# Rebuilding half of a reloaded operand on VectorE in a Strassen-Winograd MLP

## The chip, the cores and the metric

The kernel runs on one core of one Trainium2 chip. Five engines work side by side: TensorE (PE in the profile, with PEld for its weight loads), VectorE (DVE), ScalarE (ACT), GpSimd (POOL) and SyncE (SP, which here issues nearly all DMA transfers). The metric is the device time of one execution in microseconds; the figure shown for a kernel is the median over its runs.

## The reference

Two pre-normalized blocks with residuals, on x of 2048 x 1024 in bf16: a linear-attention block, and then a token-mixing MLP, whose matrix products run over the sequence. Only the MLP's second product matters here:

```
u = einsum("bsd,sf->bdf", h, w1) + b1     # first product, S = 2048 -> F = 3584
u = gelu(u)
y = einsum("bdf,fs->bds", u, w2) + b2     # second product, F = 3584 -> S = 2048
out = h + transpose(y)
```

## The kernel before

**Tiling.** The activations g = gelu(u) stay in SBUF, f16, split by feature tile: `gE` holds the even tiles of 128 features and `gO` the odd ones, each 14 tiles of 1024 columns (line 1532). The second product is done by the Winograd form of Strassen's scheme: seven products p1 to p7 of quarter size for each pair of 128-row output tiles, with moving operands that are sums of quarters of g. `gT2` is one of these, T3 = T2 - gE and T4 = gO - T2 (left columns) are two more. T2 lives in SBUF. T3 and T4 do not fit at once: they share two buffers, `gs0` and `gs1`, each half a T (7 tiles of 512 columns, 896 KB). They are computed once on VectorE (`derived`, line 1600), stored to DRAM (`parked`), and fetched again whenever needed (`reload`, line 1609).

**Two levels.** The outputs of two neighbouring pairs form a quad (class `Quad`). For a quad, products p1, p5, p2 and p3 are themselves done by a seven-product scheme (classes `Inner` and `Inner2`, i1 to i7, matmuls of 128x256), on the left operands of both pairs together; p6, p7 and p4 are done directly with matmuls of 128x512. The inner schemes leave short gaps in which their PSUM results are copied or summed, so `interleave` (line 536) weaves a direct product into each of them, in four portions: at the points named "b", "c", "2", "7", "third" and "end" it empties a list of late output steps or calls what the quad hung there.

**One quad** (`run2`, line 592) runs four interleaved stages in this order:
- in1 (inner product 1) with what is left of the last quad's p4, which reads the second half of T4. Its PE rows are psI for the inner product and psC<-gs for p4.
- in5 with p6 (rows psB<-gT). p6 accumulates onto a bank that ScalarE filled from the sums of in1 (line 523).
- in2 with p7, which reads T3 (psC<-gs).
- in3 with the first half of p4, which reads the first half of T4. `begin_next` starts the left-hand sums (rows is<-wq) for the next quad's in1.

Quads u = 1, 2 and 3 run this way; the second half of p4 of the last one runs after it, on its own.

**Order around the change.** `loads(u)` (line 1637) says when SyncE fetches what: T3 in "in3" and "in1", the first half of T4 at "p7", and its second half at "in2", just ahead of in3, right behind the two loads of the next quad's weights (`next2`, line 1630, called in line 647). A reload of a buffer waits until the products that read the old content are done. SyncE takes its queue strictly in order. VectorE and TensorE keep the order of the program in this part (class `Held`, line 222); ScalarE's order is left to the scheduler.

On VectorE, in3 consists of four sums of PSUM results into e (rows e<-psI,e; the second adds one result to both pairs) and two pairs of left-hand sums: that of in3 itself, and that of the next quad's in1. ScalarE then writes the two finished rows (line 487, wq<-e), to which POOL issues the output DMA.

In place, the even tiles of `gO` are altered early: the inner scheme's own sums (`sums2`) replace the right half of the left columns of every even tile by its difference with the left half (line 217, b12 - b11). T4 is made before that, at line 1674.

Of the kernel before, what the change touches and what calls it, by code (L numbers as in the profile page):

```python
# [10 lines left out]
P = 128  # L11
F32 = mybir.dt.float32
BF16 = mybir.dt.bfloat16
FP16 = mybir.dt.float16
ACT = mybir.ActivationFunctionType
ALU = mybir.AluOpType
# [14 lines left out]
def kernel(  # L31
# [12 lines left out]
    nc = tc.nc  # L44
# [5 lines left out]
    CW = min(BANK, D)  # L50
# [83 lines left out]
    NFP, NSP = NF // 2, NS // 2  # L134
    assert NDC == 2 and NF % 2 == 0 and NS % 2 == 0

    HW = CW // 2
# [23 lines left out]
    def load_w2(p, second, q=nc.sync):  # L161
        q.dma_start(
            (odd[p] if second else even[p % 2]),
            B_w2[:, p * 2 * P:(p + 1) * 2 * P].rearrange("(k two p) s -> p k two s", two=2, p=P)[:, :, second, :],
        )

    def first_w2(p):
        t = w_tile(wpool, WLEN)
        ots.extend(t[:, 2 * WH + o:2 * WH + o + CW] for o in (0, CW))
        even[p], odd[p] = w2_view(t[:, 0:WH]), w2_view(t[:, WH:2 * WH])  # L170
        odd[p + 4] = odd[p]
        for second in (0, 1):
            load_w2(p, second)
# [28 lines left out]
    dram = ctx.enter_context(tc.tile_pool(name="dram", bufs=1, space=bass.MemoryType.DRAM))  # L202
# [29 lines left out]
    dve, pe, act = Held(nc.vector), Held(nc.tensor), Held(nc.scalar, key="scalar")  # L232
# [267 lines left out]
    def share(sts):  # L500
        t = cpool.tile([P, 2, BANK], F32, tag="e", name="e1")
        for s, st in enumerate(sts):
            st.e = t[:, s, :]
        return t[:]

    class Quad:
# [85 lines left out]
        def run2(self, rest, nxt, load, sums, cut):  # L592
            sts = self.sts

            def starting():
                self.in1.sums(slice(2, 4))
                self.asums(5)
                self.in5 = self.inner(5)
                self.in5.sums(slice(0, 2))
                sts[0].asum(6)  # L600
                self.t1 = self.base("t1")
                for s, st in enumerate(sts):
                    st.begin(self.t1[:, s, :])

            def evac(s, dh, t):
                return lambda: sts[s].evac(0, dh, t[:, s, :])

            def every(*fs):
                return lambda: [f() for f in fs]

            def shared(st):
                self.late.pop(0)()
                dve.tensor_tensor(st.e[:], st.B[:], st.e[:], ALU.add)

            self.in1.behind = self.late
            self.interleave(
                self.in1, rest, {"b": starting, "7": lambda: self.in5.sums(slice(2, 4)), "third": sums[0]},
                (("b", None), ("7", None), ("end", None)),
            )
            load("in1")  # L620
            sts[1].asum(6)
            sums[1]()
            e = share(sts)
            in2 = Inner2(sts, 2, self.mov2, "i", self.add_to(self.t1), None)
            in2.sums(slice(0, 2))
            self.interleave(self.in5, self.steps(*[st.p6 for st in sts]), {
                "b": lambda: sts[0].asum(7), "2": lambda: sts[1].asum(7),
                "7": lambda: in2.sums(slice(2, 4)), "third": sums[2],
            })

            def third():
                self.in3 = Inner2(sts, 3, self.mov3, "i", self.add_to(e), None)
                shared(sts[0])
                evac(0, 0, self.t1)()
                self.in3.sums(slice(0, 2))

            self.interleave(in2, self.pieces(lambda st: st.p7_fill), {
                "b": every(lambda: sts[0].asum(3), sums[3]), "2": lambda: sts[1].asum(3),
                "7": lambda: load("p7"), "third": third,
                "end": lambda: self.late.append(evac(1, 0, self.t1)),  # L640
            }, (("7", None),))
            shared(sts[1])
            if cut is not None:
                sts[-1].split(cut)
                for st in sts:
                    st.fetch(1, 0)
            nxt = nxt()
            load("in2")
            p4 = self.pieces(lambda st: st.p4)

            def begin_next():
                if nxt is not None:
                    nxt.in1 = nxt.inner(1)
                    nxt.in1.sums(slice(0, 2))
                evac(0, 1, e)()

            self.interleave(self.in3, p4[:len(p4) // 2], {
                "b": lambda: self.in3.sums(slice(2, 4)), "third": begin_next,
                "end": lambda: self.late.append(evac(1, 1, e)),
            }, (("b", None), ("7", None)))  # L660
            load("in3")
            return p4[len(p4) // 2:], nxt
# [111 lines left out]
    with ExitStack() as actx:  # L774
# [21 lines left out]
        with ExitStack() as a1:  # L796
# [466 lines left out]
            for q in range(2, NVP):  # L1263
                for R in (KRun, VRun):
                    n = R(q)
# [28 lines left out]
            for b in range(NKB):  # L1294
                j0, n = b * KPB, min(KPB, ND - b * KPB)
# [237 lines left out]
    gO = gpool.tile([P, NFP, D], FP16, name="gO")  # L1533
# [44 lines left out]
    H2 = NFP // 2  # L1578
    gT2 = g2pool.tile([P, NFP, CW], FP16, name="gT2")
# [9 lines left out]
    parked = {}  # L1589

    def gs_tile(m, h):
        t = g2pool.tile([P, H2, CW], FP16, tag=f"gs{h}", name=f"gs{h}")
        gs[m, h] = t
        now = [gs.get((m, i)) for i in range(2)]
        gmov[m] = lambda k: now[k // H2][:, k % H2, :]
        return t

    gs = {}

    def derived(m, of):  # L1600
        def make(h):
            t = gs_tile(m, h)
            dve.tensor_tensor(t[:], *of(spans[h]), ALU.subtract)
            parked[m, h] = dram.tile([P, H2, CW], FP16, name=f"parked{m}{h}")
            nc.sync.dma_start(parked[m, h][:], t[:])

        return [partial(make, h) for h in range(2)]

    def reload(m, h):
        hd.dma_start(gs_tile(m, h)[:], parked[m, h][:])  # L1610

    make_t3 = derived(7, lambda sl: (gT2[:, sl, :], gE[:, sl, 0:CW]))
    make_t4 = derived(4, lambda sl: (gO[:, sl, 0:CW], gT2[:, sl, :]))
    first_w2(1)
    for p in (2, 3):
        odd[p] = odd[p + 4] = w2b.tile([P, NFP, 2 * P], BF16, tag=f"o{p}", name=f"w2o{p}")[:]
# [20 lines left out]
    def loads(u):  # L1637
        def load(at):
            last = 2 * u + 2 >= NSP
            if at == "in1":  # L1640
                if u == 1:
                    reload(7, 0)
                reload(7, 1)
                for p in (2 * u + 2, 2 * u + 3):
                    if 4 <= p < NSP:
                        load_w2(p, 1, hd)
            elif at == "p7":
                reload(4, 0)
            elif at == "in2":
                reload(4, 1)  # L1650
            elif at == "in3":
                if not last:
                    reload(7, 0)
        return load
# [70 lines left out]
```

## Time and profile before

| what | value |
|---|---|
| median of 5 runs | 563.22 us (562.88 to 564.05) |
| the profiled execution: its time, its span | 564.05 us, 562.2 us |
| TensorE busy | 552.6 us, 98% of the span, 3323 matmuls |
| VectorE busy | 427.9 us, 76%, 836 instructions |
| ScalarE busy | 291.1 us, 52% |
| granted TensorE clock | full in all slices |
| DMA moved | 77.92 MB, 139 GB/s over the span |
| reloads of gs from DRAM | 12 of 896 KB, median 5.1 us from issue to landing |
| stores of gs to DRAM | 4 of 896 KB, median 9.2 us |
| weight loads of the second product | 896 KB each, median 7.7 us (group of 12) |

The page gives busy time per engine; TensorE is the fullest. Times in the timeline are counted from the start of the span. A row of the timeline gives start, length, engine, source line (230 is the recording helper, under which most of this part stands), operation, output<-inputs, shape and how many instructions were merged; in brackets stands how long the engine was idle before it and what ended that. The second product runs from about 395 us on; quad 1 starts near 430, quad 2 near 473 and quad 3 near 514.

### The profile page before, as it was taken

The numbers are of one execution on the slowest core, as the hardware profiler recorded it, in microseconds if no ns is written. First come the engines' busy times: TensorE is split into PE (matmuls) and PEld (weight loads), VectorE is DVE, ScalarE is ACT, GpSimd is POOL, SyncE is SP. The second block draws the span as 40 slices with busy tenths as digits, with TensorE's granted clock in tenths as the row PEclk, the third lists the DMA queues.
The fourth block names the chain that finished last, engine by engine and source line by source line (L and its number), as shares of the span: only waits on it lengthen the run. The fifth ranks groups of instructions, "written<-read, shape, count | busy, mean of one in ns | idle before, by whom it ended". The sixth has DMA issues, their size and how long they took to land.

```text
span 562.2 us, 8812 instructions
## 1 busy us (share of the span) xinstructions
PE 552.6 (98%) x3323; PEld 316.3 (56%) x3339; DVE 427.9 (76%) x836; ACT 291.1 (52%) x617; POOL 28.1 (5%) x38
## 2 busy tenths in 40 slices
PE   8999999999999999999999999999999999998997
PEld 3444444454444444456666766666445666666665
DVE  6898888544777688889989789888997878648643
ACT  5747777766767877645546465564211312413313
POOL 1000000000000000000000000000002103102112
PEclk9999999999999999999999999999999999999999
DMA  9933342115774761103140340422969749849336
GB/s 294 305 75 76 76 91 41 19 40 199 221 207 130 245 196 76 75 1 103 50 149 22 129 151 1 150 66 66 234 203 273 220 139 294 209 128 275 87 92 134
DMA packets 84203, 77.92 MB, mean 139 GB/s; under 512 B 15666, under 2 KB 76096, under 8 KB 84160
## 3 DMA queue, kind: packets, MB, share of 16 engines
q1 hardware_dynamic: 79104, 72.76, 43.0%
q0 software_dynamic: 4384, 3.95, 4.8%
q10 hardware_dynamic: 672, 0.66, 0.4%
q8 instruction: 26, 0.43, 0.3%
q14 instruction: 17, 0.14, 0.1%
HBM read 61.62 MB, written 12.58 MB: 132 GB/s over the span
## 4 chain that ended last, share of the span: by engine, by line
PE 91%; DMA 5%; DVE 2%; SPq 1%; issue 1%; ACT 0%; DVEq 0%; ACTq 0%
PE psI L230 23%; PE acc_t L230 18%; PE psC L230 14%; PE psB L230 8%; PE psC L940 4%; PE psB L940 4%; DMA gs<-parked 4%; PE psA L940 4%; PE psB L342 2%; PE psA L342 2%; PE acc_t L1226 2%; PE psE L940 2%; PE psC L342 2%; PE acc_t L864 2%; DMA x_sb<-in_A_x_dram 1%; PE psA L230 1%
## 5 line engine op out<-in xcount | busy, mean ns | idle before, releaser
L230 PEld LDWEIGHTS <-is 128*128 128x128 f16 x736 | 71.8, 98 | 31.1 <-DVE hi L230 0.4
L230 PEld LDWEIGHTS <-sa 128*128 128x128 f16 x606 | 59.2, 98 | 27.1
L230 PEld LDWEIGHTS <-wq 128*128 128x128 bf16 (+1 forms) x496 | 48.5, 98 | 30.0 <-issue 2.9
L230 PE MATMUL acc_t<-wo_sb,pqT 128*128 128x512 f16 x256 | 55.6, 379 | 0.0
L484 POOL DMA_DIRECT2D out_dram<-wq x30 | 26.2, 935 | 528.8 <-ACT wq L487 498.1
L230 PE MATMUL acc_t<-xnT,wq_sb 128*128 128x512 bf16 x188 | 43.1, 379 | 0.2
L230 PEld LDWEIGHTS <-pqT 128*128 128x128 bf16 x256 | 25.0, 98 | 30.5 <-issue 0.6
L193 DVE TENSOR_SCALAR e_sb<-e_sb 128x512 bf16<-128x512 bf16 x64 | 18.6, 290 | 28.8 <-ACT e_sb L189 28.2
L230 DVE TENSOR_TENSOR t<-psI,t 128x256 f32<-128x256 f32 (+1 forms) x45 | 20.8, 475 | 22.2 <-PE psI L230 20.9
L189 ACT ACTIVATE e_sb<-acc_t 128x512 bf16<-128x512 f32 x40 | 23.9, 597 | 24.5 <-PE acc_t L230 12.0
L230 PE MATMUL psC<-gs,wq 128*128 128x512 f16 x140 | 34.1, 379 | 1.7 <-DMA gs<-parked 1.7
L940 PEld LDWEIGHTS <-xs 128*128 128x128 f16 x208 | 20.0, 98 | 23.3 <-DVE xs L926 1.3
L230 PEld LDWEIGHTS <-wq_sb 128*128 128x128 bf16 x192 | 18.5, 98 | 23.0 <-issue 1.3
L230 PE MATMUL psC<-hT,sa 128*128 128x512 f16 x112 | 31.2, 379 | 0.0
L230 PE MATMUL psI<-hi,is 128*128 128x256 f16 x200 | 30.0, 273 | 0.0
L230 PE MATMUL psB<-hT,sa 128*128 128x512 f16 x112 | 29.7, 379 | 0.0
L230 DVE BATCH_NORM_STATS2 hst<-acc_t 128x6 f32<-128x512 f32 x32 | 21.4, 692 | 9.1 <-ACT h_bf L230 8.9
L940 PE MATMUL psA<-wkv,xnT 128*128 128x512 bf16 x99 | 26.4, 379 | 0.3
L940 PEld LDWEIGHTS <-xnT 128*128 128x128 bf16 x156 | 15.3, 98 | 18.5 <-issue 0.2
L230 DVE TENSOR_TENSOR e<-psI,es 128x256 f32<-128x256 f32 x20 | 8.5, 425 | 21.8 <-PE psI L230 21.8
L230 PE MATMUL psC<-hT,wq 128*128 128x512 f16 x96 | 24.6, 379 | 0.0
L230 ACT CAST h_bf<-acc_t 128x512 bf16<-128x512 f32 x32 | 18.4, 582 | 11.8 <-PE acc_t L230 11.1
(227 smaller groups left out, 1090.5 us busy)
## 6 DMA issues: line engine op xcount, KB each, us to landing
wq<-in_B_w_dram SPq DMA_DIRECT2D x14, 1024.0 KB, 7.9
wq<-in_B_w_dram SPq DMA_DIRECT2D x12, 896.0 KB, 7.7
gs<-parked SPq DMA_DIRECT2D x12, 896.0 KB, 5.1
xr<-in_A_x_dram SPq DMA_DIRECT2D x16, 256.0 KB, 5.5
rdb<-rd_dram SPq DMA_DIRECT2D x32, 128.0 KB, 3.9
out_dram<-h_bf SPq DMA_DIRECT2D x16, 256.0 KB, 2.0
x_sb<-in_A_x_dram SPq DMA_DIRECT2D x15, 256.0 KB, 3.1
out_dram<-wq POOLq DMA_DIRECT2D x30, 128.0 KB, 5.8
```

Of the source, the lines that this page charges most:

```text
L189: pin(nc.scalar.activation(e_sb[:], src, ACT.Exp))
L193: pin(nc.vector.tensor_scalar(e_sb[:], e_sb[:], 1.0, PHI_EPS, ALU.min, ALU.add))
L230: return (lambda *a, **kw: pin(op(*a, **kw))) if self.always or getattr(Held, self.key) else op
L342: pe.matmul(ps[:, cols], lhsT=lhs[:, k, :], rhs=mv(k)[:, cols], start=(start and k == 0), stop=(k == self.nk - 1), skip_group_check=True,)
L484: nc.gpsimd.dma_start(to, ot[:, a:b], accum_op=ALU.add)
L864: mm = nc.tensor.matmul(pp[:, 0:CW], lhsT=xnT[:, kt, i * P:(i + 1) * P], rhs=wkv[:, kt, c * CW:(c + 1) * CW], start=(kt == 0), stop=(kt == ...
L940: pin(nc.tensor.matmul(ps[:], lhsT=lhs[:, k, :], rhs=rhs[:, k, :], start=(start and k == 0), stop=(k == hk2 - 1), skip_group_check=True,))
L1226: nc.tensor.matmul(qp[:, 0:SW], lhsT=wq_sb[:, kt, j * P:(j + 1) * P], rhs=xnT[:, kt, u * SW:(u + 1) * SW], start=(kt == 0), stop=(kt == ND ...
```

## The change

The second half of T4 is no longer stored and reloaded. For each quad it is recomputed on VectorE from `gO` and `gT2`, into the same buffer gs1, in two parts inside in3: tiles 7 to 9 at its point "2" and tiles 10 to 13 at its point "7". A part is one subtraction, and one addition that puts back gO's left half in the even tiles, which `sums2` had subtracted. The first half of T4 and both halves of T3 are reloaded as before. The first quad's T4, made at line 1674, is computed as before, and only its first half is stored.

```diff
             self.interleave(self.in3, p4[:len(p4) // 2], {
-                "b": lambda: self.in3.sums(slice(2, 4)), "third": begin_next,
+                "b": lambda: self.in3.sums(slice(2, 4)), "2": lambda: load("t4a"), "7": lambda: load("t4b"),
+                "third": begin_next,
                 "end": lambda: self.late.append(evac(1, 1, e)),
...
-    def derived(m, of):
+    def derived(m, of, park=(0, 1)):
         def make(h):
             t = gs_tile(m, h)
             dve.tensor_tensor(t[:], *of(spans[h]), ALU.subtract)
-            parked[m, h] = dram.tile([P, H2, CW], FP16, name=f"parked{m}{h}")
-            nc.sync.dma_start(parked[m, h][:], t[:])
+            if h in park:
+                parked[m, h] = dram.tile([P, H2, CW], FP16, name=f"parked{m}{h}")
+                nc.sync.dma_start(parked[m, h][:], t[:])
...
+    def remake_t4(second):
+        t, k = gs[4, 1], H2 + second * H2 // 2
+        n = NFP - k if second else H2 // 2
+        o = slice(k - H2, k - H2 + n)
+        dve.tensor_tensor(t[:, o, :], gO[:, k:k + n, 0:CW], gT2[:, k:k + n, :], ALU.subtract)
+        k += k % 2
+        even_k = slice(k - H2, o.stop, 2)
+        dve.tensor_tensor(
+            t[:, even_k, HW:CW], t[:, even_k, HW:CW], gO[:, k:H2 + o.stop:2, 0:HW], ALU.add,
+        )
...
-    make_t4 = derived(4, lambda sl: (gO[:, sl, 0:CW], gT2[:, sl, :]))
+    make_t4 = derived(4, lambda sl: (gO[:, sl, 0:CW], gT2[:, sl, :]), (0,))
...
             elif at == "in2":
-                reload(4, 1)
+                gs_tile(4, 1)
+            elif at in ("t4a", "t4b"):
+                remake_t4(at == "t4b")
```

## The prediction

> **What bounds the kernel.** I read the page first: TensorE (PE) is busy 98% of the span, and the chain that ended last lies on PE for 91% of it. So only a hole in PE's own stream can be won. Then I asked who PE waits for from 395 us on, in the second MLP product, the only part that the change touches. The answer is one line (total, times, longest):
>
> ```profile
> PE psC L230 <- DMA gs<-parked: 2.7, 2, 1.7
> ```
>
> Two waits for reloads of gs, and nothing else. The timeline of PE shows where (start, length, idle before):
>
> ```profile
> 473.17 0.93 PE L230 MATMUL psI<-gE,wq 128*128 128x256 f16 x7
> 475.13 1.02 PE L230 MATMUL psC<-gs,w2o 128*128 128x512 f16 x4 [1.03 <-DMA gs<-parked]
> 475.99 0.93 PE L230 MATMUL psI<-gi,is 128*128 128x256 f16 x7
> ...
> 513.89 0.93 PE L230 MATMUL psI<-gE,wq 128*128 128x256 f16 x7
> 516.50 1.02 PE L230 MATMUL psC<-gs,wq 128*128 128x512 f16 x4 [1.68 <-DMA gs<-parked]
> 517.36 0.93 PE L230 MATMUL psI<-gi,is 128*128 128x256 f16 x7
> ```
>
> The psC groups are the first four steps of product 4 on the **second half of T4**, woven into the next quad's first inner product. Idle in brackets leaves out PE's pipeline, so I count from starts. The chain has 14 matmuls of 128x256 in 1.53 us, so seven take 0.765 us, and psC could start at 473.17 + 0.765 = 473.94 and at 513.89 + 0.765 = 514.66. It starts **1.19 and 1.84 us** later: 3.03 us are open. The last quad's second half is used at its end, with no wait on a reload.
>
> Why the reload is late shows on SyncE's queue:
>
> ```profile
> 461.95 2.64 SPq L230 DMA_DIRECT2D wq<-in_B_w_dram  x2
> 464.65 8.28 SPq L230 DMA_DIRECT2D gs<-parked  x2
> ```
>
> It is issued at 464.65, behind two weight loads of 896 KB of which one had just left; the chain of waits gives it 10.43 us, and 11.09 us a quad later. Reloads with no weight load just ahead of them land in 4.6 to 5.6 us.
>
> **What goes.** Three reloads and one store of 896 KB, and two PE waits. By the Trainium skill ("DMA: Bandwidth & Descriptors", Anatomy of one DMA; Rules for kernel authors) a transfer costs some 2.0 us + bytes/436e3, and is to be issued early and waited for late. Its fit, made for another DMA path, gives 4.1 us as an estimate for 917,504 bytes: landed at 468.8, five us early, nothing to win, and the change would only load VectorE. The trace has 10.43 and 11.09 us under load, so I take the 3.03 us. The store (issued after 424) delays no PE instruction: PE has no wait between 395 and 475. SyncE loses four issues of about 0.33 us; its other loads keep their order and mostly wait for PE, so nothing there is won.
>
> **What comes.** Per quad, four VectorE (DVE) subtractions and additions, of 1,536, 256, 2,048 and 512 half-precision elements, in the third inner product. The order of the built program shows the first two right behind the e sum of 468.43, the other two behind the second sum of the pair at 469.78, and PE's order unchanged. The same operands were subtracted once already, in f16 throughout:
>
> ```profile
> 420.25 2.03 DVE L1603 TENSOR_TENSOR gs<-gO,gT 128x3584 f16<-128x3584 f16 x1 [0.68 <-PE psC L342]
> ```
>
> Groups by shape give 0.618 us for 896 and 1.083 for 1,792, also where a source is cut in runs of 256 (gO<-gO 1.092): 0.519 ns an element and 0.153 us fixed. So 0.95, 0.29, 1.22, 0.42 us. What counts is when the next one starts:
>
> ```profile
> 468.43 0.42 DVE L230 TENSOR_TENSOR e<-psI,e 128x256 f32<-128x256 f32 x1
> 469.78 1.22 DVE L230 TENSOR_TENSOR e<-psI,e 128x512 f32<-128x512 f32 x2 [0.94 <-PE psI L230]
> 471.96 0.42 DVE L230 TENSOR_TENSOR e<-psI,e 128x256 f32<-128x256 f32 x1 [0.95 <-PE psI L230]
> 472.43 0.63 DVE L230 TENSOR_TENSOR is<-wq 128x896 f16<-128x896 bf16 x1
> 473.09 0.63 DVE L230 TENSOR_TENSOR is<-is,wq 128x896 f16<-128x896 f16 x1
> 473.63 0.42 DVE L230 TENSOR_TENSOR e<-psI,e 128x256 f32<-128x256 f32 x1
> 473.97 0.62 DVE L230 TENSOR_TENSOR is<-wq 128x896 f16<-128x896 bf16 x1
> 474.50 0.62 DVE L230 TENSOR_TENSOR is<-wq,is 128x896 f16<-128x896 bf16 x1
> ...
> 480.18 0.42 DVE L230 TENSOR_TENSOR t<-psI,es 128x256 f32<-128x256 f32 x1 [0.74 <-PE psI L230]
> ...
> 481.59 0.42 DVE L230 TENSOR_TENSOR t<-psI,es 128x256 f32<-128x256 f32 x1
> ```
>
> The is of 474.50 starts 0.09 before the end of the one ahead; that of 473.09, which reads what 472.43 wrote, 0.03 after. The additions read what the subtractions wrote, so part one takes 0.95 + 0.03 + 0.29 - 0.08 = 1.19 and part two 1.22 + 0.03 + 0.42 - 0.08 = 1.59: **2.78 us a quad**. The skill ("VectorE: DVE Perf Modes", The DRAIN you can't avoid) says the next operation starts only when the pipe is empty, without overlap: the full durations and gaps would be 0.2 more, 2.94. The rows overlap; I take 2.78, with 2.3 (elements alone) and 2.94 as ends.
>
> **Who waits for it.** First, PE for T4 itself: part two ends near 472.7, wanted at 473.94. Second, what is queued behind on VectorE:
> - The two inner sums of 469.78 move to 469.97 and 470.8; PE's last inner group at 472.40 needs the second, done by 471.2.
> - The sum of 471.96 moves to 472.7 and the is pair to 473.05 and 473.7, done by 474.35. PE wants it at 474.80, after four psC steps of 0.216 us.
> - ScalarE (ACT):
>
> ```profile
> 473.36 1.50 ACT L487 ACTIVATE wq<-e,b_sb 128x512 bf16<-128x512 f32 x2 [5.56 <-DMA out_dram<-wq]
> 474.76 0.36 ACT L270 COPY psI<-psI 128x256 f32<-128x256 f32 x1
> ...
> 482.09 0.38 ACT L523 COPY psB<-t 128x256 f32<-128x256 f32 x1 [1.08 <-DVE t L230]
> ```
>
> L270 now runs behind both output evacuations, and PE's next inner group needs it. With that order PE could start only at 475.2 and 0.4 us would go. In the new order the second evacuation stands behind L270: first one 473.36 to 474.08, L270 474.18 to 474.54, before 474.80. Cost nothing.
> - The tightest: the sum at 481.59 and L523 behind it feed the product-6 matmul:
>
> ```profile
> 483.50 2.10 PE L230 MATMUL psB<-gT,sa 128*128 128x512 f16 x9
> ```
>
> L523 ends at 482.47, so 1.03 us are spare; PE now comes 1.19 earlier. VectorE has idle 0.94 + 0.95 + 0.74, three lost overlaps of 0.08 and 0.12 before 472.43 = 2.99 us between 468.43 and 481.59. It takes the 2.78 and runs without a gap, 0.2 earlier at the end. 1.03 + 0.2 covers 1.19, with nothing to spare; allowing for semaphores I book 0.1 us of new wait. A quad later the idles are 0.94, 0.96, 0.60, 0.84, plus 0.32: 3.66 - 2.78 + 1.03 = 1.91 against 1.84, 0.05 booked. If the cover is gone, each 0.1 us more on VectorE costs 0.1 us at each of the two places.
> - Last quad: sums wait for PE 0.94, 0.96 and 0.99 us, 3.1 with overlaps, more than 2.78; the last sum (555.48) stays in place, and the first evacuation (554.51) ends by 556.0, before the next starts. Cost nothing.
>
> **Sum.** 3.03 - 0.15 = 2.9 us off the span of 562.2. The profiled execution took 564.05, 1.85 outside the span, which stays; the median of the five runs is 563.22. 563.22 - 2.9 = **560.3 us**.
>
> **Rivals.**
> 1. VectorE's unbroken queue becomes the bound at the product-6 matmul. For it: no margin. If the four cost 0.5 us more (contention, waits between them), 1.0 comes back: 561.3.
> 2. Another wait takes the hole: the first evacuation's output buffer (its wait above is 5.56 us on an output DMA) or the weight load that ends at 513.70. For it: both sit right beside the hole. Against: the reload left the same queue, so they should land no later. If only about 0.5 us is left at each place: 562.2.
> 3. Slower: VectorE takes the four at one element per cycle, as the f32 rows do (0.69 for 512 against 0.42 for 256: 1.05 ns an element). 4,352 x 1.05 + 4 x 0.15 = 5.2 us a quad. The place is the same psB matmul; break-even there is 2.99 + 1.03 = 4.0 us in the first quad and 4.7 in the second. PE then comes 1.2 and 0.5 us later than before, and the end some 1.7: 563.22 + 3.4 = 566.6. Against it stands the L1603 row, 3,584 elements in 2.03 us.
> 4. The change doesn't do what it says, for instance a wait of the new operations on a release that comes late: the old tile's last reader is the psC group of 462.52, long done. Counted with 2.
>
> **Chances.** Forecast (2.2 us or more won) 0.72; rival 1 0.12; rivals 2 and 4 0.08; rival 3, or VectorE in the way otherwise, 0.08. The range goes from 559.8 (no new wait, and 0.4 us of spread) to 562.2 (rivals 1 and 2). No change, within 0.2%, is 562.1 to 564.3: faster 0.82, within 0.10, slower 0.08.
>
> **What will show it.** PE's waits from 395 us on no longer name gs<-parked; the distance from the psI group before to the psC group is 0.77 us, not 1.96 and 2.61. VectorE runs unbroken from the first remake to the t sums; the four take 0.95, 0.29, 1.22 and 0.42 us. I am wrong if PE shows a wait for VectorE or ScalarE at psI<-gi,is or at the first psB group of over 0.3 us, or if the remake rows are much longer.

## The result, and the profile after

| kernel | median | range | runs |
|---|---|---|---|
| before | 562.99 us | 562.18 to 566.38 | 49 |
| after | 560.93 us | 560.63 to 563.98 | 28 |

The ratio is 0.9966, 95% interval 0.9959 to 0.9973: 1.5 to 2.3 us faster, 2.06 by the medians, where 2.9 was forecast. The profiled execution of the changed kernel took 560.78 us, with a span of 559.0.

From 395 us on PE now waits for nothing that the profile shows: no wait names gs<-parked, and none has taken its place. This is the timeline of the changed kernel around the first of the two places (start, length, engine, line, operation; idle before and its releaser in brackets), and PE's rows of the second place at its end:

```profile
467.63 0.42 DVE L230 TENSOR_TENSOR e<-psI,e 128x256 f32<-128x256 f32 x1
467.97 0.95 DVE L230 TENSOR_TENSOR gs<-gO,gT 128x1536 f16<-128x1536 f16 x1
468.95 0.29 DVE L230 TENSOR_TENSOR gs<-gs,gO 128x256 f16<-128x256 f16 x1
469.16 1.21 DVE L230 TENSOR_TENSOR e<-psI,e 128x512 f32<-128x512 f32 x2
470.29 1.22 DVE L230 TENSOR_TENSOR gs<-gO,gT 128x2048 f16<-128x2048 f16 x1
471.54 0.42 DVE L230 TENSOR_TENSOR gs<-gs,gO 128x512 f16<-128x512 f16 x1
471.88 0.42 DVE L230 TENSOR_TENSOR e<-psI,e 128x256 f32<-128x256 f32 x1
...
472.33 0.72 ACT L487 ACTIVATE wq<-e,b_sb 128x512 bf16<-128x512 f32 x1 [5.32 <-DVE e L230]
472.38 0.93 PE L230 MATMUL psI<-gE,wq 128*128 128x256 f16 x7
473.14 1.03 PE L230 MATMUL psC<-gs,w2o 128*128 128x512 f16 x4
473.34 0.36 ACT L270 COPY psI<-psI 128x256 f32<-128x256 f32 x1 [0.29 <-PE psI L230]
...
473.90 0.72 ACT L487 ACTIVATE wq<-e,b_sb 128x512 bf16<-128x512 f32 x1 [0.21 <-DVE e L230]
474.00 0.93 PE L230 MATMUL psI<-gi,is 128*128 128x256 f16 x7
...
481.04 0.38 ACT L523 COPY psB<-t 128x256 f32<-128x256 f32 x1 [1.08 <-DVE t L230]
481.51 2.10 PE L230 MATMUL psB<-gT,sa 128*128 128x512 f16 x9
...
511.90 0.93 PE L230 MATMUL psI<-gE,wq 128*128 128x256 f16 x7
512.67 1.03 PE L230 MATMUL psC<-gs,wq 128*128 128x512 f16 x4
```

Read it from PE: psC follows the psI group by 0.76 us (472.38, 473.14) and 0.77 us (511.90, 512.67), where it was 1.96 and 2.61. On DVE, the rows from 467.63 to 471.88 have no idle in brackets: the four new operations fill the gaps in which the e sums had waited for PE. On ACT, the copy L270 stands ahead of the second output evacuation (473.90); in the kernel before it stood behind both. L523 ends at 481.42, and the psB group that needs it starts at 481.51.

SyncE's queue, same stretch, has nothing behind the two weight loads until the next reload of T3:

```profile
461.16 2.64 SPq L230 DMA_DIRECT2D wq<-in_B_w_dram  x2
471.81 0.34 SPq L230 DMA_DIRECT2D gs<-parked  x1
```

The end of the kernel is the one place that got worse. The timeline of the kernel before there:

```profile
554.51 0.72 ACT L487 ACTIVATE wq<-e,b_sb 128x512 bf16<-128x512 f32 x1 [4.62 <-DVE e L230]
555.27 3.20 PE L230 MATMUL psC<-gs,w2o 128*128 128x512 f16 x21
555.53 0.86 POOL L484 DMA_DIRECT2D out_dram<-wq  x1 [4.58 <-ACT wq L487]
558.17 0.84 ACT L487 ACTIVATE wq<-psC,b_sb 128x384 bf16<-128x384 f32 x2 [0.50 <-PE psC L230]
```

and of the changed kernel:

```profile
551.38 1.49 ACT L487 ACTIVATE wq<-e,b_sb 128x512 bf16<-128x512 f32 x2 [5.32 <-DVE e L230]
551.45 3.20 PE L230 MATMUL psC<-gs,w2o 128*128 128x512 f16 x21
552.40 1.76 POOL L484 DMA_DIRECT2D out_dram<-wq  x2 [5.27 <-ACT wq L487]
554.35 0.58 ACT L487 ACTIVATE wq<-psC,b_sb 128x384 bf16<-128x384 f32 x1 [0.50 <-PE psC L230]
555.58 0.37 ACT L487 ACTIVATE wq<-psC,b_sb 128x128 bf16<-128x128 f32 x1 [0.65 <-DMA out_dram<-wq]
```

Count from the last psC group. The first output row used to be evacuated 0.76 us ahead of it (554.51, 555.27) and is now 0.07 ahead (551.38, 551.45), because the recomputation holds up its sum. Its output DMA is issued 0.95 us behind the psC start instead of 0.26. The kernel has four output buffers, so the fifth evacuation of this end, the last 128 columns, takes the buffer of the first. It waited for nothing before (the two of 558.17 run back to back) and now waits 0.65 us for that DMA. The chain of waits of the changed kernel passes through it:

```profile
552.40 3.07 DMA out_dram<-wq
...
555.58 0.38 ACT wq L487
```

From the last psC start to the end of the span it was 562.2 - 555.27 = 6.93 us, and is 559.0 - 551.45 = 7.55: 0.62 given back in this profile.

### The profile page after: what moved, and what is told of

It reads as the page before. It is cut to its first block, busy times and chain, and to the rows that moved or that the text cites. A ratio compares the mean times of both kernels' runs of the same rounds, so it can differ in the third digit from the quotient of the medians.

```text
span 559.0 us, 8813 instructions
## 1 busy us (share of the span) xinstructions
PE 551.5 (99%) x3323; PEld 315.9 (57%) x3339; DVE 435.1 (78%) x848; ACT 291.2 (52%) x617; POOL 28.1 (5%) x38
## 4 chain that ended last, share of the span: by engine, by line
PE 71%; issue 19%; POOL 4%; DMA 3%; DVE 2%; SPq 1%; ACT 0%; POOLq 0%; DVEq 0%; ACTq 0%
PE acc_t L230 18%; PE psI L230 14%; PE psC L230 8%; PE psB L230 5%; PE psC L941 4%; PE psB L941 4%; PE psA L941 4%; POOL out_dram L484 4%; PE acc_t L1227 2%; PE psE L941 2%; PE psC L342 2%; PE psA L342 2%; PE acc_t L865 2%; DMA x_sb<-in_A_x_dram 1%; DMA wq<-in_B_w_dram 1%
## 5 line engine op out<-in xcount | busy, mean ns | idle before, releaser
L230 ACT COPY psI<-psI 128x256 f32<-128x256 f32 x50 | 18.0, 360 | 11.7 <-PE psI L230 9.8
```

What stands on the lines that cost most here:

```text
L230: return (lambda *a, **kw: pin(op(*a, **kw))) if self.always or getattr(Held, self.key) else op
```

## The experiments

Two lengths from each profile do most of the work. The **stretch** runs from quad 1's first psB group of nine (442.78 in the kernel before) to quad 3's (524.87); both places lie in it. (The expectations of e9 to e11 count from an earlier psB group, at 403.43, so their stretch is some 39.4 us longer.) The **tail** runs from the last psC start to the end of the span. "Before again" is a second profile of the unaltered kernel.

Each ratio is to runs of the kernel before made beside that kernel. Their median was 562.81 us for e1 to e4, 562.70 for e5 to e8 and 563.15 for e9 to e12, so medians of different groups do not compare to better than some tenths; ratios and stretches do.

| kernel | stretch | tail | median | ratio to before, interval |
|---|---|---|---|---|
| before | 82.09 | 6.93 | 562.99 | |
| before again (e9) | 81.04 | 6.91 | 562.36, one run | |
| after | 79.05 | 7.55 | 560.93 | 0.9966, 0.9959 to 0.9973 |
| e1 last quad reloads | 79.05 | 7.06 | 560.31 | 0.9953, 0.9938 to 0.9968 |
| e2 store kept | 79.06 | 7.28 | 560.73 | 0.9960, 0.9945 to 0.9976 |
| e3 no fill | 80.27 | 7.11 | 561.26 | 0.9970, 0.9961 to 0.9980 |
| e4 one subtraction twice | 80.96 | 8.55 | 563.91 | 1.0019, 1.0010 to 1.0028 |
| e5 no fill, new ScalarE order | 79.06 | 7.15 | 561.46 | 0.9979, 0.9970 to 0.9988 |
| e6 old ScalarE order | 80.94 | 7.42 | 563.53 | 1.0016, 1.0005 to 1.0027 |
| e7 before, new ScalarE order | 81.38 | 6.85 | 563.53 | 1.0017, 1.0008 to 1.0027 |
| e8 reload earlier | 89.52 | 6.97 | 571.61 | 1.016, 1.014 to 1.018 |
| e10 as e5, quads 1 and 2 only | 79.05 | 7.12 | 560.73 | 0.9960, 0.9948 to 0.9973 |
| e11 as e6, quads 1 and 2 only | 80.94 | 7.56 | 563.38 | 1.0001, 0.9992 to 1.0010 |
| e12 own output buffer | 79.05 | 7.36 | 560.78 | 0.9963, 0.9950 to 0.9976 |

Kernels e5 to e8 hold ScalarE's order in the last quad too. That moves a copy (L403) ahead there, and the piece between stretch and tail grows from 30.41 to 31.31 us: 0.9 us of their time is a side effect. Kernels e10 and e11 repeat e5 and e6 without it.

### e1: the last quad reloads, quads 1 and 2 recompute

```diff
-    make_t4 = derived(4, lambda sl: (gO[:, sl, 0:CW], gT2[:, sl, :]), (0,))
+    make_t4 = derived(4, lambda sl: (gO[:, sl, 0:CW], gT2[:, sl, :]))
...
             elif at == "in2":
-                gs_tile(4, 1)
+                if last:
+                    reload(4, 1)
+                else:
+                    gs_tile(4, 1)
             elif at in ("t4a", "t4b"):
-                remake_t4(at == "t4b")
+                if not last:
+                    remake_t4(at == "t4b")
```

> The changed kernel, but the last quad (u = 3) reloads its second half of T4 from DRAM as before; quads 1 and 2 rebuild it. The store of that half is kept. Theory (the rebuild in the last quad delays the first of the two output rows, whose buffer the very last evacuation of 128 columns needs; this cost about 0.65 us at the end): the last evacuation no longer waits for an output DMA, and the distance from the start of the last psC group of 21 to the end of the span goes back from 7.55 us to about 6.9; the time is 0.6 us below that of the changed kernel, about 560.3 us. Rival (the tail of the changed kernel's profile is chance, or an output DMA that lands differently each time): the time stays at 560.9, and the distance too.

560.31 us. The stretch is that of the changed kernel, and the last two evacuations run back to back again:

```profile
554.44 0.88 ACT L487 ACTIVATE wq<-psC,b_sb 128x384 bf16<-128x384 f32 x2 [0.50 <-PE psC L230]
```

So the recomputation in the last quad, where nothing had waited for the reload, wins nothing and costs the tail, which is 7.06 us here. On the same chip e2, which recomputes in all three quads, took 560.55 to 560.98 us, and e1 560.24 to 560.52: the two ranges do not meet. This version has the lowest time of all.

### e2: the store is kept

```diff
-    make_t4 = derived(4, lambda sl: (gO[:, sl, 0:CW], gT2[:, sl, :]), (0,))
+    make_t4 = derived(4, lambda sl: (gO[:, sl, 0:CW], gT2[:, sl, :]))
```

> The changed kernel, but the second half of the first T4 is still stored to DRAM, where nobody reads it. Theory (the store delays nothing that TensorE waits for): the same time as the changed kernel, 560.9 us within 0.3. Rival (part of the gain comes from 896 KB less on the queues around 425 to 435 us): between 561.2 and 562.

560.73 us (560.55 to 560.98), as expected, with the stretch unchanged: the dropped store is worth nothing that shows. The tail, 7.28 us, is 0.27 shorter than in the changed kernel's profile, though nothing there differs; its last evacuation waited 0.45 us for its buffer, not 0.65. So the 0.62 us that the tail lost is 0.35 in this profile.

### e3, e5 and e10: the second half of T4 is not filled at all

```diff
-                gs_tile(4, 1)
-            elif at in ("t4a", "t4b"):
-                remake_t4(at == "t4b")
+                halves = (gs[4, 0], gs[7, 1])
+                gmov[4] = lambda k: halves[k // H2][:, k % H2, :]
```

> Neither reload nor rebuild: the second half of product 4 reads what lies in the buffer, the second half of T3, so that half of T4 is left out of the result. ScalarE has the old order here, with both output evacuations ahead of the copy that starts the next inner product. Theory (the reload wait is all that could be won, VectorE's four operations cost nothing on the way but 0.65 us at the end, and with the old ScalarE order 0.4 to 1 us of the hole stays behind that copy): no PE wait for a DMA; psI to second psI about 2.0 us in quad 2 (2.82 before, 1.62 after); about 560.5 to 561.0 us. Rival (VectorE's operations cost more than the profile shows): clearly below the changed kernel, 559.9 or less.

e3 does less than the changed kernel and still took longer: 561.26 us, above the expected 561.0. Beside it e2, which rebuilds that half, took 560.73, and 10 of e3's 12 runs lie above the longest of e2. Its timeline shows who is late:

```profile
472.66 0.62 DVE L230 TENSOR_TENSOR is<-wq 128x896 f16<-128x896 bf16 x1 [0.65 <-DMA wq<-in_B_w_dram]
...
474.36 0.72 ACT L487 ACTIVATE wq<-e,b_sb 128x512 bf16<-128x512 f32 x1 [1.23 <-DVE e L230]
474.99 0.36 ACT L270 COPY psI<-psI 128x256 f32<-128x256 f32 x1
...
475.41 0.92 PE L230 MATMUL psI<-gi,is 128*128 128x256 f16 x7 [0.82 <-ACT psI L270]
```

Without the new work on VectorE the scheduler left ScalarE in its old order. The second evacuation waits for the last e sum, held up here by a weight load for 0.65 us; the copy L270 stands behind it, and PE behind L270. The stretch is 1.22 us longer than the changed kernel's, 0.98 of it at this first place and 0.24 at the second. To part the order from the fill, e5 and e10 skip the fill and keep the changed kernel's order:

```diff
-            act.copy(self.b, self.a)
+            (hs if Quad.order and self.mov is Quad.mov1_2 else act).copy(self.b, self.a)
...
-                "end": lambda: self.late.append(evac(1, 1, e)),
+                "end": lambda: self.late.append(lambda: sts[1].evac(0, 1, e[:, 1, :], q=hs if nxt is not None else nc.scalar)),
...
```

(This is e10; the edit that skips the fill is that of e3. `hs` keeps the program's order on ScalarE; e5 has it in the last quad too, and for an evacuation of the second inner product.)

> Neither reload nor rebuild (the second half of T4 is left out of the result, as in e3_no_fill), and ScalarE held to the order of the changed kernel: the copy that starts the next inner product ahead of the second output evacuation. Theory (e3_no_fill was slow because of ScalarE's order alone): no PE wait in quads 2 and 3, psI to second psI 1.62 us as in the changed kernel, and no wait in the tail: 560.3 us within 0.3, as e1_last_reload, so the rebuild itself costs nothing in quads 1 and 2. Rival (PE waits there for something else, the weight load or the left-hand sums): still 561 us or more.

> Left out: the second half of T4 is neither reloaded nor recomputed (the products that use it read half a tile of T3 instead). ScalarE keeps the changed kernel's order everywhere, in the last quad too. Theory (the rebuild itself costs PE nothing in quads 1 and 2, and only the late output buffer in the last quad): the stretch between the first psB groups of quads 1 and 2 is 118.4 us as in the changed kernel, the tail behind the last psC start is 7.1 us or less instead of 7.55, and the time is 560.3 us (560.1 to 560.6). Rival (the rebuild takes PE time on VectorE that the holes hide): 559.5 us or less, with a stretch below 118.2.

Both stretches are those of the changed kernel to 0.01 us (79.06, 79.05), so the recomputation costs PE nothing in quads 1 and 2. The tail of e10 is 7.12 us. e5's 561.46 us missed its 560.3 by the 0.9 us of the side effect and 0.3 more. e10's median, 560.73, lies 0.13 us above the band that was expected, and five runs from 560.47 to 561.60 do not set it apart from the changed kernel.

### e4: the first subtraction done twice

```diff
+        if not second:
+            dve.tensor_tensor(t[:, o, :], gO[:, k:k + n, 0:CW], gT2[:, k:k + n, :], ALU.subtract)
```

> The changed kernel with the first subtraction of each quad (1,536 elements, 0.95 us) done twice. Theory (VectorE runs without a gap from the rebuild to the sums that feed product 6, and the copy behind them ends only 0.1 us ahead of TensorE): some 0.8 us of new wait at the first psB group of quads 2 and 3, and some 0.9 more at the end: about 563.0 us, as before the change. Rival (VectorE still has slack): 560.9 to 561.3.

563.91 us, above the expected 563.0. PE's waits in this kernel, from 390 us on (total, times, longest):

```profile
PE psI L230 <- DVE is L230: 0.7, 2, 0.4
PE psB L230 <- ACT psB L523: 0.4, 2, 0.2
```

The stretch grew by 80.96 - 79.05 = 1.91 us, 0.96 and 0.95 at the two places, for two more subtractions of 0.97 us (the pair takes 1.94). VectorE's cover in the changed kernel is used up: what is added to it comes out at PE almost in full, at both places. The tail took another 1.00 us (8.55 against 7.55), again through the output buffer, whose wait is now 1.62 us.

### e6 and e11: the changed kernel in ScalarE's old order

```diff
-            act.copy(self.b, self.a)
+            (hs if Quad.order and self.mov is Quad.mov1_2 else act).copy(self.b, self.a)
...
-                "end": lambda: self.late.append(evac(1, 1, e)),
+                "end": lambda: sts[1].evac(0, 1, e[:, 1, :], q=hs if nxt is not None else nc.scalar),
...
```

(This is e11; e6 has the order in the last quad too.)

> The changed kernel with ScalarE held to the order before the change: both output evacuations ahead of the copy that starts the next inner product. Theory (the second evacuation waits for the last sum of the third inner product, which ends near 473.8, and takes 0.72 us, so the copy ends near 475.0 and PE starts 1.0 us later in each of quads 2 and 3): 562.5 to 563.0 us, nearly all of the gain lost, with PE waiting for the copy of line 270. Rival (the order matters little beside the reload): 561.0 to 561.8.

> The changed kernel, with ScalarE's old order (both output evacuations ahead of the copy L270) in quads 1 and 2 only. Theory (the second evacuation waits for the last sum on VectorE, so the copy behind it comes 0.95 us late at each of two places): PE waits for ScalarE at psI<-gi,is twice, some 0.8 us idle each, stretch 120.3 us, time 562.8 us (562.5 to 563.1), as slow as the kernel before. Rival (the loss that an earlier run of this kind showed lay in its side effect in the last quad): 561.2 us or less.

The timeline of e11:

```profile
473.63 0.72 ACT L487 ACTIVATE wq<-e,b_sb 128x512 bf16<-128x512 f32 x1 [5.32 <-DVE e L230]
475.21 0.72 ACT L230 ACTIVATE wq<-e,b_sb 128x512 bf16<-128x512 f32 x1 [0.86 <-DVE e L230]
475.84 0.36 ACT L230 COPY psI<-psI 128x256 f32<-128x256 f32 x1
...
476.25 0.93 PE L230 MATMUL psI<-gi,is 128*128 128x256 f16 x7 [0.78 <-ACT psI L230]
```

The stretch is 1.89 us longer than with the new order, in both kernels. With the recomputation in front of it, the last e sum comes late, so the second evacuation idles 0.86 us for it, and the copy for PE stands behind. e6 took 563.53 us, 0.9 of it the side effect. e11 took 563.38 us, no different from the kernel before (ratio 1.0001) and 0.3 us above the expected band; its profile was already 1.3 us later than the changed kernel's at the start of the stretch, for a reason that stays open. Without the new order on ScalarE the change would have won nothing.

### e7: the kernel before in the new ScalarE order

The same ScalarE edit as in e5, on the kernel before.

> The kernel before the change with the new ScalarE order alone. Theory (before, PE waits for the reload until after the copy is done in either order): no difference, 562.8 to 563.1 us, and PE still waits for gs<-parked 2.7 us. Rival (the order alone makes part of the gain): 562.2 or less.

563.53 us, of which 0.9 is the side effect. The stretch is 81.38: PE still waits for gs<-parked, 2.0 us in all, where 2.7 was expected. The new order alone removes no wait while the reload is late.

### e8: the reload issued between the two weight loads

```diff
-        for p in (2 * u, 2 * u + 1):
-            load_w2(p, 0, hd)
+        load_w2(2 * u, 0, hd)
+        if load is not None:
+            load("in2")
+        load_w2(2 * u + 1, 0, hd)
...
```

(Made on the kernel before, with the new ScalarE order.)

> The kernel before the change with the new ScalarE order, and the reload of the second half of T4 issued between the two weight loads of the next quad instead of behind both; nothing is rebuilt. Theory (the queue is full: what goes ahead delays what comes behind): the reload lands in time and PE's wait for gs goes, but the second weight load lands some 2 us later, near 475, the left-hand sums (rows is<-wq) wait for it and PE waits for them: 562.5 to 563.5 us. Rival (the order of the queue alone could have given the gain): 560.3 to 561 us.

571.61 us: 8.1 slower than e7, which differs in nothing but the place of the reload, and far above the 562.5 to 563.5 that was expected. The wait for gs is gone, and VectorE's left-hand sums wait for a weight load instead:

```profile
473.35 1.03 PE L230 MATMUL psC<-gs,w2o 128*128 128x512 f16 x4
...
475.78 0.62 DVE L230 TENSOR_TENSOR is<-wq 128x896 f16<-128x896 bf16 x1 [3.97 <-DMA wq<-in_B_w_dram]
...
477.12 0.94 PE L230 MATMUL psI<-gi,is 128*128 128x256 f16 x7 [2.74 <-DVE is L230]
477.89 1.44 PE L230 MATMUL psI<-gE,wq 128*128 128x256 f16 x7
479.12 1.91 PE L230 MATMUL psC<-gs,w2o 128*128 128x512 f16 x4
```

In the kernel before that sum started at 472.43 without a wait. The chain of waits gives the second weight load 11.71 us here and 13.01 a quad later, where the kernel before has 10.43 and 11.09 for the reload: of the two orders tried, each leaves one of the transfers late, the one issued last. Leaving the reload out helps both.

Waiting is not all of the 8.1 us. The psI group follows psC by 3.77 us (473.35, 477.12) and by 5.10 a quad later, against 0.86 in the changed kernel, so the two holes are 2.91 and 4.24 us, 7.15 together, where e7 has 2.33: 4.8 us more. The other 3.3 us are slower matmuls behind each hole, as the last two rows show (seven in 1.44 us instead of 0.93, four in 1.91 instead of 1.03). The granted clock in the profile is 1.00 from 460 to 473, 0.50 from 478.5 to 481.5, and 1.00 again from 482 on; a quad later it is 0.50 from 523 to 525. Behind the shorter holes of the kernel before, 1.19 and 1.84 us, it stays at 1.00 (475 to 481 and 516 to 522).

### e9: the kernel before, profiled again

> The kernel before, unaltered, profiled a second time. Theory (the reload stall is a landing time on a loaded queue and so differs from one execution to the next): PE again waits for gs<-parked at the same two places, for a total between 1.5 and 2.7 us and not for anything else from 395 us on; the stretch from the first psB group of quad 1 to that of quad 2 (403 to 525 us) takes 120.4 to 121.5 us. Rival (the stall is fixed): 2.7 us and 121.4 us again, within 0.1.

```profile
472.63 0.93 PE L230 MATMUL psI<-gE,wq 128*128 128x256 f16 x7
474.45 1.02 PE L230 MATMUL psC<-gs,w2o 128*128 128x512 f16 x4 [0.89 <-DMA gs<-parked]
...
513.21 0.93 PE L230 MATMUL psI<-gE,wq 128*128 128x256 f16 x7
514.91 1.02 PE L230 MATMUL psC<-gs,wq 128*128 128x512 f16 x4 [0.78 <-DMA gs<-parked]
```

The distances are 1.82 and 1.70 us; less the 0.765 that seven matmuls take, the hole is 1.06 + 0.94 = 2.0 us; the wait that the profile names is 1.7, within the expected 1.5 to 2.7. In the first profile the hole was 3.03, and in e7 it was 2.33 (its stretch less 79.05). It is not fixed: it is how late two transfers land in that execution. The chains of waits give the two reloads 10.43 + 11.09 us in the first profile, 10.28 + 10.53 in e7 and 10.29 + 10.19 in e9. These sums fall by 0.71 and 1.04 us from the first, the holes by 0.70 and 1.03.

### e12: a buffer of its own for the last 128 columns

```diff
-            ot = ots.pop(0)
-            ots.append(ot)
+            ot = cpool.tile([P, b - a], BF16, tag="last", name="last")[:] if a else ots.pop(0)
+            ots.extend([] if a else [ot]); ot = ot if a else ot[:, a:b]
...
```

> The changed kernel, with a buffer of its own for the last evacuation of 128 columns; the rebuild stays in all three quads. Theory (what the change gives back in the last quad is the wait of that evacuation for a late output DMA that holds its buffer): the wait is gone, the tail behind the last psC start is 6.9 to 7.1 us instead of 7.55, time 560.3 us (560.1 to 560.6). Rival (the tail is late because VectorE or ScalarE is late at the end, whatever the buffer): tail 7.5 us, 560.9 us as the changed kernel.

Half of this held. The wait for the buffer is gone; in the timeline of e12 the last evacuation starts 3.38 us behind the psC start of 551.44, instead of 4.13:

```profile
554.82 0.36 ACT L487 ACTIVATE last<-psC,b_sb 128x128 bf16<-128x128 f32 x1
```

But the tail is still 7.36 us. The DMA issues show part of the reason. This is the end of e12 (KB each, median from issue to landing):

```profile
out_dram<-wq SPq DMA_DIRECT2D x1, 96.0 KB, 2.1
out_dram<-last SPq DMA_DIRECT2D x1, 32.0 KB, 1.8
```

and of e1:

```profile
out_dram<-wq SPq DMA_DIRECT2D x1, 96.0 KB, 1.7
out_dram<-wq SPq DMA_DIRECT2D x1, 32.0 KB, 1.6
```

The evacuation comes 0.75 us earlier, but the write of its 32 KB is issued only 0.45 us earlier, at 555.77, because SyncE is issuing the write of 96 KB until 555.68. It then took 1.8 us to land, where the changed kernel has 1.5. That it shares the DMA engines with the late accumulating writes fits, but was not tried by itself. And 7.36 is no shorter than the 7.28 of e2, which has no such buffer, so what the buffer gains is not clear of the scatter between profiles. The time, 560.78 us (560.33 to 562.12), does not separate e12 from the changed kernel.

## Why the prediction was right, and where it was not

**The hole goes: right.** The two waits were the reload, and with them gone the stretch shortened by 82.09 - 79.05 = 3.04 us against the profile on which the sum of 3.03 was made. e10 has the same stretch with neither reload nor recomputation.

**The four operations: right.** Forecast 0.95, 0.29, 1.22 and 0.42 us; the rows show the same four numbers. From start to start the two parts take 1.19 us (467.97 to 469.16) and 1.59 (470.29 to 471.88), the 2.78 that was booked. The section of the Trainium skill from which the prediction took its 2.94 ("VectorE: DVE Perf Modes", The DRAIN you can't avoid) itself adds that a next operation which is not held starts earlier; the rows agree, with 0.08 us of overlap at 469.16. From the start of the e sum at 467.63 to that at 471.88 is 4.25 us; in the kernel before it was 471.96 - 468.43 = 3.53, with PE's waits in it. They ran at the rate of the L1603 row, so rival 3 had no ground.

**The tightest point: right.** "Nothing to spare" is 0.09 us between L523 and psB. The 0.15 us booked for new waits was not used. That each further 0.1 us on VectorE would cost 0.1 at each of the two places is what e4 measured: 1.91 us for 1.94.

**ScalarE's order: right in use, mis-sized.** The old order was put at 0.4 us; e11 shows 1.89 us over two places, 0.95 each. The working let the second evacuation follow the first at once, and left out that it waits for the last e sum, which the change itself makes late.

**The last quad, "Cost nothing": wrong.** Two of its statements held: the last sum stayed 0.2 us behind the psC start, and the first evacuation ended before the next began. The step stopped there. It did not follow the evacuation on to POOL's output DMA, and from that to the buffer which the fifth evacuation needs. Measured: 0.62 us of tail in one profile and 0.35 in that of e2; in e1 the wait is gone and 0.13 remains. That e1's median of 560.31 equals the 560.3 forecast for the whole is chance: against the 562.81 of its own group it won 2.5 us, not 2.9.

**The 3.03 us as a typical hole: too large.** It came from one execution, which took 564.05 us, 0.8 above the median of the runs then at hand; part of that lies ahead of the stretch, which starts at 442.78 there and at 442.24 in e9. The three profiles with the reload in its place have 3.03, 2.33 and 2.0 us, 2.45 on average. That less some 0.5 of tail (7.55 and 7.28 in two profiles, against 6.93) is 2.0 us, and 2.06 was measured. The forecast subtracted an unusually large stall from a usual time. Of the 0.84 us by which 2.9 overshot, the tail and the size of the hole explain about half each, with the unused 0.15 against them; three profiles fix the average hole to no better than some tenths.

**Rivals.** None came true as told. The time lies within the range of 559.8 to 562.2, but the gain of 2.06 us (1.5 to 2.3) is just under the "2.2 us or more" to which the forecast gave 0.72. The second (another wait takes the hole) was nearer than its chance suggests: in quads 1 and 2 a wait of 0.95 us a place for ScalarE was avoided only by the scheduler's new order, and the wait for an output buffer did appear, in the last quad.

## What to carry to other kernels

A stall on a transfer is a landing time, and here it varied from 2.0 to 3.03 us between executions: profile it more than once before subtracting it from a median. A wait can also cost more than its own length: in e8 each hole of 2.9 us or more was followed by a stretch at half the granted clock. Where an engine is filled to its last gap, follow each delayed result through its evacuation and its output DMA to the buffer that the DMA holds, above all in the last iteration, where no later work hides it. And apply a change only in the iterations where the wait exists: leaving the last quad on the reload kept the whole gain, and gave the lowest time.

## What the hardware showed beyond expectation

- The same reload, issued at the same place in the same queue, left PE waiting for 3.03 us in one execution and for 2.0 in another, and its landing times differ by as much.
- Putting it one place forward in the queue cost 8.1 us. PE's two holes grew from 2.33 to 7.15 us, and behind each of them the granted clock was 0.50 for about 3.4 us, which took 3.3 us more in all. Behind holes of 1.19 and 1.84 us the clock stayed at 1.00.
- A kernel that left out the recomputation was slower than one that made it (e3 561.26, e2 560.73 us): work on VectorE had changed the scheduler's order on ScalarE. The old order cost PE 1.22 us over two places in e3, and 1.89 with the recomputation (e6, e11).
- The evacuation of the last 128 columns came 0.75 us earlier with its own buffer, and the kernel ended only 0.2 us earlier (tail 7.36 against 7.55): its write was issued 0.45 us earlier and took 1.8 us to land instead of 1.5, and that of the write before it 2.1 instead of 1.9.
